# Keeping the split weights of the first MoE batch in DRAM and loading them for the other three

## The chip, the cores and the metric

The kernel runs on one core of one Trainium2 chip. A time is the device time of one execution in microseconds (us); what counts is the median over several executions.

## The reference

Three stages run one after the other. Attention with mixed heads makes x of 1792 tokens by 768 features. A dense "MoE" layer then computes g(x w_in) w_out with a hidden width of 2048, and a soft-MoE layer with 32 slots and 8 experts works on its output. The change lies in the second stage:

```python
def _moe_ref(x, w_in, w_out):
    h = x @ w_in            # 1792x768 @ 768x2048
    g = h - np.tanh(h)
    return g @ w_out        # 1792x2048 @ 2048x768
```

## The kernel before

**Attention** (`talking_heads`) runs until about 526 us. Beside it, the weights w_in and w_out, which arrive as 64-bit floats, are turned into 32-bit floats and stored in DRAM as 16 blocks `wi[f]` and 16 blocks `wo[f]`, each 128 partitions by 768 floats (384 KB).

**The MoE stage** (`moe_and_slots`) works on 4 batches of 448 tokens, and for each on the 16 blocks f of the hidden width: 64 steps t = 16b + f. A matmul is to be as exact as 32-bit floats need, but TensorE takes the fast format fp32r, so each operand is split into a high half (ScalarE copies it, rounded to fp32r) and a low half (what is left, by a subtraction), and three products are added: high by high, low by high, high by low. Both layers of a step therefore have 18 matmuls of 448 columns each.

- `stage1(t)` multiplies x by block `wi[f]` into the PSUM tile `hp` (L653); `gate(t)` computes g from it on ScalarE (`sq`, `qd`, `g`, L665 to L667) and VectorE (L668 to L673).
- `ready2(t)` splits `wo[f]` and g; `stage2(t)` multiplies them into the six accumulators `acc` (L686).
- `load_i` and `load_o` bring a block from DRAM on SyncE's queue (L600, L606). `split_to` makes the halves: the high one on ScalarE (L612), the low one on GpSimd for weights and on VectorE for g and x (L613). So each batch loads and splits the same 32 blocks again: 64 loads of `wi`, 64 of `wo`, 128 splits.

Every engine runs its instructions in the order in which the program writes them. In the middle of a batch a step t is written as: `load_i(t+2)`, `split_i(t+1)` (its names in the profile are `wir`, `wih`, `wil` for the raw block and its halves), `stage1(t)`, `gate(t)`, `stage2(t-2)`, then `ready2(t)` with the split of `wo` (`wor`, `woh`, `wol`) and `load_o(t+2)`. TensorE thus alternates stage1(t), stage2(t-2), stage1(t+1), stage2(t-1). The raw block of `wi` has one buffer, that of `wo` two, and each half has two.

At the start of batches 1 to 3 TensorE also finishes the batch before: `prep_logits`, `prep_transpose`, `prep_mix` and their like compute the slots of the soft MoE, mixed with the first four steps. At the end of a batch `split_x` splits the six blocks of the next x (`xh` on ScalarE, `xl` on VectorE).

From step 24 on, each step with a free tile also loads a piece of the expert weights (`load_expert`, L575, 1536 KB): seven pieces in steps 24 to 30, four in steps 53 to 56, two after the last stage1. The remaining experts are loaded while the last part (`hidden`, `finish`, `slot_out`, `output`) runs, from 1056 us to the end.

Of the kernel before, what the change touches and what calls it, by code (L numbers as in the profile page):

```python
# [16 lines left out]
NB, NH, SEQ, HD = 4, 12, 448, 64  # L17
# [23 lines left out]
def bits(ap):  # L41
    return ap.bitcast(FP32)
# [469 lines left out]
        pass  # L512


def moe_and_slots(tc, ident, xd, wi, wo, phi, w1, w2, out, box):
    nc = tc.nc
    NT, DM = out.shape
    KD = DM // 128
    NF = len(wi)
# [9 lines left out]
    steps = [(b, f) for b in range(NB) for f in range(NF)]  # L529
    NST = len(steps)  # L530
# [63 lines left out]
    raw_i, raw_o, wih, xraw, xhl, gt, ready, acc = {}, {}, {}, {}, {}, {}, {}, {}  # L594
    x2T, x2n, lp, es_in, runs = {}, {}, {}, {}, {}

    def load_i(t):
        if t < NST:
            a = xp.tile([128, DM], FP32, tag="wir", name="wir", bufs=1)
            nc.sync.dma_start(out=a, in_=wi[steps[t][1]])  # L600
            raw_i[t] = a

    def load_o(t):
        if t < NST:
            a = gt_p.tile([128, DM], FP32, tag="wor", name="wor")
            nc.sync.dma_start(out=a, in_=wo[steps[t][1]])  # L606
            raw_o[t] = a

    def split_to(pool, tag, n, src, lo_eng):
        h = pool.tile([128, n], F32R, tag=tag + "h", name=tag + "h", bufs=2)  # L610
        l = pool.tile([128, n], F32R, tag=tag + "l", name=tag + "l", bufs=2)
        nc.scalar.activation(out=h, in_=src, func=ACTF.Copy)  # L612
        lo_eng.tensor_tensor(out=l, in0=src, in1=bits(h), op=ALU.subtract)  # L613
        return h, l
# [24 lines left out]
    def stage1(t, mid=None):  # L639
        b, f = steps[t]  # L640
        if b and f == LAG - 1:
            hp = box["acc"].tile([128, SEQ], FP32, tag=f"a{KD - 1}", name="hp")
        else:
            hp = ph.tile([128, SEQ], FP32, tag="h", name="hp")
        wh, wl = wih.pop(t)
        n = 0
        for c in range(KD):
            if mid and c == KD // 2:
                mid()
            cs = slice(c * 128, (c + 1) * 128)  # L650
            xh, xl = xhl[b][c]
            for w, x in ((wh, xh), (wl, xh), (wh, xl)):
                nc.tensor.matmul(hp, lhsT=w[:, cs], rhs=x, start=(n == 0), stop=(n == 3 * KD - 1))  # L653
                n += 1
        return hp

# [19 lines left out]
    def stage2(t):  # L676
        b, f = steps[t]
        pa = box["acc"]
        if f == 0:
            for c in range(KD):  # L680
                acc[c] = pa.tile([128, SEQ], FP32, tag=f"a{c}", name="acc")
        wh, wl, gh, gl = ready.pop(t)
        for c in range(KD):
            cs = slice(c * 128, (c + 1) * 128)
            for i, (w, g) in enumerate(((wh, gh), (wl, gh), (wh, gl))):
                nc.tensor.matmul(  # L686
                    acc[c], lhsT=w[:, cs], rhs=g, start=(f == 0 and i == 0), stop=(f == NF - 1 and i == 2))
# [155 lines left out]
    pend = []  # L843

    def pop2():
        stage2(pend.pop(0))
        for u in pend[:2]:
            ready2(u)

    for t in range(NST):  # L850
# [55 lines left out]
    b = NB - 1  # L906
# [158 lines left out]
def fused_kernel(  # L1065
# [61 lines left out]
```

## Time and profile before

| | |
|---|---|
| median of 3 runs | 1159.91 us |
| lowest, highest | 1156.6, 1160.01 us |
| the profiled execution | 1161.43 us |
| its span in the profile | 1159.7 us |
| TensorE busy, share of the span | 1089.1 us, 94% |
| VectorE, ScalarE, GpSimd busy | 776.1, 655.2, 493.9 us |
| GpSimd: low halves of `wi`, of `wo` | 64 of 2.03 us, 64 of 1.90 us on average |
| bytes moved by DMA, mean rate | 221.08 MB, 191 GB/s |

The profile shows one execution. PE is TensorE's matmul, DVE VectorE, ACT ScalarE, POOL GpSimd, SP SyncE; "SPq" and "ACTq" are DMAs issued by SyncE and ScalarE. A busy TensorE is the bound only where its matmuls follow each other at their shortest distance, so the distance of one step to the next says more than the busy share.

### The profile page before, as it was taken

How to read it: one execution, taken by the hardware profiler on the slowest of the kernel's cores; microseconds unless marked ns; L12 is line 12 of the kernel's file. 1: busy time of each engine (PE TensorE's matmuls, PEld its weight loads, DVE VectorE, ACT ScalarE, POOL GpSimd, SP SyncE). 2: the span in 40 equal slices, each digit the busy share in tenths (PEclk: the TensorE clock that was granted, in tenths of full speed). 3: DMA queues.
4: the chain of work that ended last, by engine and by line, in shares of the span. 5: the costliest groups of instructions: out<-in, count | busy, mean ns of one | idle time of the engine just before them, and what ended most of it. 6: DMA issues, size and time to landing. Idle time of an engine off the chain costs nothing.

```text
span 1159.7 us, 20722 instructions
## 1 busy us (share of the span) xinstructions
PE 1089.1 (94%) x7208; PEld 871.5 (75%) x7208; DVE 776.1 (67%) x1428; ACT 655.2 (56%) x1399; POOL 493.9 (43%) x582
## 2 busy tenths in 40 slices
PE   7899999999998999999999899998999999999995
PEld 5677777777776777768888779886899879886443
DVE  6567666876767567636777787678966787775013
ACT  4777867867777677755454445445455554442022
POOL 1354455445644355545544345544455445450000
PEclk7899999999999899999999999999999999998898
DMA  5789868986899666544423224783333325627998
GB/s 121 193 233 238 239 188 243 253 228 201 231 240 233 205 204 216 178 151 140 150 95 110 69 82 157 270 293 103 131 111 107 97 68 195 240 83 272 365 388 308
DMA packets 160443, 221.08 MB, mean 191 GB/s; under 512 B 59124, under 2 KB 133172, under 8 KB 159828
## 3 DMA queue, kind: packets, MB, share of 16 engines
q1 hardware_dynamic: 160032, 219.65, 61.0%
q8 instruction: 58, 0.95, 0.3%
q14 instruction: 45, 0.37, 0.1%
q0 software_dynamic: 48, 0.10, 0.0%
q10 hardware_dynamic: 260, 0.01, 0.0%
HBM read 147.96 MB, written 23.59 MB: 148 GB/s over the span
## 4 chain that ended last, share of the span: by engine, by line
PE 47%; DVE 16%; DMA 14%; issue 8%; POOL 7%; ACT 7%; SPq 0%; POOLq 0%; DVEq 0%; ACTq 0%
PE tm L344 9%; PE pm L308 9%; PE acc L686 6%; PE vx L363 5%; DMA wir<-wi 5%; PE hp L653 5%; POOL wil L613 4%; DMA D<-S 3%; DVE qd L670 3%; PE sc L286 3%; PE sc L287 3%; DVE qd L668 2%; PE h L952 2%; DMA f<-in_moe_w_out_dram 2%; POOL wol L613 2%
## 5 line engine op out<-in xcount | busy, mean ns | idle before, releaser
L344 PEld LDWEIGHTS tm<-wk,e 120*112 120x112 f32 (+1 forms) x1440 | 171.7, 178 | 94.5 <-issue 55.9
L613 POOL TENSOR_TENSOR wil<-wir,wih 128x768 fp32r<-128x768 f32 x64 | 129.7, 2027 | 171.1 <-ACT wih L612 167.0
L344 PE MATMUL tm<-wk,e 120*112 120x120 f32 (+1 forms) x1440 | 180.2, 269 | 13.2 <-ACT aT L347 8.9
L310 DVE TENSOR_REDUCE mx<-pm 120x1 f32<-120x448 f32 x180 | 112.1, 623 | 113.3 <-PE pm L308 110.7
L334 POOL TENSOR_SCALAR wk<-wpost,rv 120x120 f32<-120x120 f32 x180 | 124.7, 693 | 137.5 <-PE tm L344 80.5
L308 PE MATMUL pm<-D,wpre 120*120 120x448 f32 x360 | 170.8, 556 | 7.6 <-DMA D<-S 2.5
L613 POOL TENSOR_TENSOR wol<-wor,woh 128x768 fp32r<-128x768 f32 x64 | 121.4, 1896 | 106.1 <-ACT woh L612 106.1
L347 ACT ACTIVATE aT<-tm 112x480 f32<-112x480 f32 x180 | 104.3, 580 | 103.6 <-PE tm L344 102.6
L653 PE MATMUL hp<-xh,wil 128*128 128x448 f32 x384 | 143.8, 374 | 7.3 <-POOL wil L613 7.0
L653 PE MATMUL hp<-xl,wih 128*128 128x448 f32 x384 | 141.8, 369 | 6.2 <-DVE xl L636 6.2
L653 PE MATMUL hp<-xh,wih 128*128 128x448 f32 x384 | 142.3, 371 | 4.4 <-ACT x2n L722 4.4
L686 PE MATMUL acc<-gh,woh 128*128 128x448 f32 x384 | 140.9, 367 | 0.0
L686 PE MATMUL acc<-gh,wol 128*128 128x448 f32 x384 | 140.6, 366 | 0.0
L686 PE MATMUL acc<-gl,woh 128*128 128x448 f32 x384 | 140.5, 366 | 0.0
L317 ACT ACTIVATE e<-pm,mx 120x448 f32<-120x448 f32 x180 | 112.5, 625 | 6.9 <-DVE rv L329 4.9
L668 DVE SCALAR_TENSOR_TENSOR qd<-qd,sq 128x448 f32<-128x448 f32 x64 | 57.5, 898 | 80.0 <-ACT qd L666 79.8
L612 ACT ACTIVATE gh<-g 128x448 fp32r<-128x448 f32 x64 | 36.8, 575 | 128.9 <-DVE g L673 127.1
L291 ACT ACTIVATE S<-sc 120x448 f32<-120x448 f32 (+1 forms) x188 | 100.7, 542 | 14.9 <-PE sc L287 7.2
L323 POOL TENSOR_SCALAR rv<-ss 120x1 f32<-120x1 f32 x180 | 46.3, 257 | 127.6 <-ACT e L317 119.8
L613 DVE TENSOR_TENSOR gl<-g,gh 128x448 fp32r<-128x448 f32 x64 | 73.0, 1144 | 36.2 <-ACT gh L612 36.2
L286 PE MATMUL sc<-khi,qT 128*120 128x448 f32 (+1 forms) x192 | 89.2, 464 | 7.4 <-ACT S L291 6.4
L653 PEld LDWEIGHTS hp<-xh,wil 128*128 128x128 f32 x384 | 72.4, 189 | 22.6 <-POOL wil L613 17.3
(135 smaller groups left out, 2017.6 us busy)
## 6 DMA issues: line engine op xcount, KB each, us to landing
ex<-in_moe_w_dram SPq DMA_DIRECT2D x32, 1536.0 KB
D<-S SPq DMA_DIRECT2D x172, 210.0 KB
wir<-wi SPq DMA_DIRECT2D x64, 384.0 KB
wor<-wo SPq DMA_DIRECT2D x64, 384.0 KB
f<-in_moe_w_in_dram SPq DMA_DIRECT2D x32, 384.0 KB
f<-in_moe_w_out_dram SPq DMA_DIRECT2D x32, 384.0 KB
wi<-fa SPq DMA_DIRECT2D x32, 192.0 KB
wo<-fa SPq DMA_DIRECT2D x32, 192.0 KB
```

The source lines that it names most:

```text
L286: nc.tensor.matmul(x[:ni], lhsT=qT[n][:, h, :ni], rhs=kT_hi[b, p][:, e, :], start=True, stop=False)
L291: nc.scalar.activation(out=S_t[n][:ni, h, :], in_=x[:ni], func=ACTF.Copy)
L308: nc.tensor.matmul(x[:r], lhsT=wpre[:r, :m, :], rhs=D_t.pop(s)[:r], start=True, stop=True)
L310: nc.vector.tensor_reduce(out=mx[:r], in_=x[:r], op=ALU.max, axis=AX.X, negate=True)
L317: nc.scalar.activation(out=e[:r], in_=pp_t.pop(s)[:r], func=ACTF.Exp, bias=mx_t.pop(s)[:r], accum_out=ss[:r])
L334: nc.gpsimd.tensor_scalar(out=wk[:r], in0=wpost[:r], scalar1=ss_t.pop(s)[:r], scalar2=None, op0=ALU.mult)
L344: nc.tensor.matmul(x[:, c, :, :m], lhsT=e[:r, c * JP:(c + 1) * JP], rhs=wk[:r, :, :m], start=True, stop=True)
L347: nc.scalar.activation(out=attn_t[n][:, :, :, c0:c0 + m], in_=x[:, :, :, :m], func=ACTF.Copy)
L613: lo_eng.tensor_tensor(out=l, in0=src, in1=bits(h), op=ALU.subtract)
L653: nc.tensor.matmul(hp, lhsT=w[:, cs], rhs=x, start=(n == 0), stop=(n == 3 * KD - 1))
L668: nc.vector.scalar_tensor_tensor(out=qd, in0=qd, scalar=TG_E, in1=sq, op0=ALU.add, op1=ALU.mult)
L686: nc.tensor.matmul(acc[c], lhsT=w[:, cs], rhs=g, start=(f == 0 and i == 0), stop=(f == NF - 1 and i == 2))
```

## The change

For batch 0 the raw block is loaded straight into the place of the low half of a tile that holds both halves. ScalarE writes the high half beside it, and GpSimd overwrites the raw block by the low half. One step later `save` stores both halves (768 KB) in DRAM, from ScalarE's queue. In batches 1 to 3 `load_i` and `load_o` bring both halves in one transfer of 768 KB, and no weight is split. The tile of `wi` has three buffers, that of `wo` two. Because a `wo` tile is now read by TensorE itself, its load is written behind `stage2(t-2)`, whose tile it takes, and no longer in `ready2`. In batches 1 to 3 the low half of g moves from VectorE to GpSimd.

```diff
+    WI_BUFS, WO_BUFS = 3, 2
+    unsaved = []
     def load_i(t):
         if t < NST:
-            a = xp.tile([128, DM], FP32, tag="wir", name="wir", bufs=1)
-            nc.sync.dma_start(out=a, in_=wi[steps[t][1]])
-            raw_i[t] = a
+            b, f = steps[t]
+            wih[t] = xp.tile([128, 2, DM], F32R, tag="wi", name="wi", bufs=WI_BUFS)
+            if b:
+                nc.sync.dma_start(out=bits(wih[t]), in_=wis[f])
+            else:
+                nc.sync.dma_start(out=bits(wih[t][:, 1]), in_=wi[f])
...
+    def split_to(w, kept):
+        raw = bits(w[:, 1])
+        nc.scalar.activation(out=w[:, 0], in_=raw, func=ACTF.Copy)
+        nc.gpsimd.tensor_tensor(out=w[:, 1], in0=raw, in1=bits(w[:, 0]), op=ALU.subtract)
+        unsaved.append((kept, w))
+
+    def save():
+        while unsaved:
+            kept, w = unsaved.pop(0)
+            nc.scalar.dma_start(out=kept, in_=bits(w))
     def split_i(t):
-        if t < NST:
-            wih[t] = split_to(xp, "wi", DM, raw_i.pop(t), nc.gpsimd)
+        if t < NF:
+            split_to(wih[t], wis[t])
     def ready2(t):
         if t in gt:
-            ready[t] = split_to(gp, "wo", DM, raw_o.pop(t), nc.gpsimd) + split_to(gp, "g", SEQ, gt.pop(t), nc.vector)
-            load_o(t + 2)
+            if t < NF:
+                split_to(woh[t], wos[t])
+            src = gt.pop(t)
...
+            nc.scalar.activation(out=h, in_=src, func=ACTF.Copy)
+            (nc.gpsimd if steps[t][0] else nc.vector).tensor_tensor(out=l, in0=src, in1=bits(h), op=ALU.subtract)
+            ready[t] = woh.pop(t), h, l
...
     def pop2():
-        stage2(pend.pop(0))
+        t = pend.pop(0)
+        stage2(t)
+        load_o(t + 2)
         for u in pend[:2]:
             ready2(u)
...
+        save()
         if t > 1:
             load_i(t + 2)
             split_i(t + 1)
```

`load_o` is changed like `load_i`, `stage1` and `stage2` read the halves out of the one tile, and `wis` and `wos` are 16 new DRAM blocks each. Three pieces of the engines' order show where the steps went. In each, the numbers behind a name count the program's buffers; a number right behind `wi`, `wo`, `wis` or `wos` in a source or target in DRAM is the block f.

ScalarE in the middle of batch 0, from the split of `wo` block 7 on. Before:

```order
L612 ACTIVATE woh_7429<-wor_7307 128x768
L612 ACTIVATE gh_7433<-g_7401 128x448
L612 ACTIVATE wih_7441<-wir_7374 128x768
L665 ACTIVATE sq_7464<-hp_7445 128x448
L666 ACTIVATE qd_7465<-sq_7464,tshift_6722 128x448
L667 ACTIVATE g_7466<-hp_7445 128x448
```

and now:

```order
L619 ACTIVATE wo_7440<-wo_7440 128x768
L639 ACTIVATE gh_7444<-g_7412 128x448
L626 DMA wis8_109<-wi_7324 128x1536
L626 DMA wos7_124<-wo_7440 128x1536
L619 ACTIVATE wi_7387<-wi_7387 128x768
L683 ACTIVATE sq_7473<-hp_7454 128x448
L684 ACTIVATE qd_7474<-sq_7473,tshift_6754 128x448
L685 ACTIVATE g_7475<-hp_7454 128x448
```

Two stores stand between the high half of g and the split of the next `wi` block. The second stores the `wo` tile whose low half GpSimd has just been given to make.

SyncE in the middle of batch 0, with the `wo` loads of blocks 6 to 8. Before:

```order
L606 DMA wor_7240<-wo6_91 128x768
L627 DMA xr_7242<-xd1_66 128x2688
L600 DMA wir_7244<-wi7_76 128x768
L606 DMA wor_7307<-wo7_92 128x768
L600 DMA wir_7309<-wi8_77 128x768
L606 DMA wor_7372<-wo8_93 128x768
```

and now:

```order
L615 DMA wo_7377<-wo6_91 128x768
L606 DMA wi_7387<-wi9_78 128x768
L615 DMA wo_7440<-wo7_92 128x768
L606 DMA wi_7450<-wi10_79 128x768
L615 DMA wo_7503<-wo8_93 128x768
L606 DMA wi_7513<-wi11_80 128x768
```

Measured in blocks, the `wi` loads run two blocks further ahead of the `wo` loads than they did.

SyncE where the first expert pieces are loaded, in batch 1. Before:

```order
L600 DMA wir_8612<-wi10_79 128x768
L606 DMA wor_8675<-wo10_95 128x768
L575 DMA ex_8677<-in_moe2_w1_dram 128x3x1024
L600 DMA wir_8679<-wi11_80 128x768
L606 DMA wor_8742<-wo11_96 128x768
L575 DMA ex_8744<-in_moe2_w1_dram 128x3x1024
```

and now:

```order
L604 DMA wi_8540<-wis10_111 128x1536
L613 DMA wo_8591<-wos8_125 128x1536
L575 DMA ex_8597<-in_moe2_w1_dram 128x3x1024
L604 DMA wi_8599<-wis11_112 128x1536
L613 DMA wo_8650<-wos9_126 128x1536
L575 DMA ex_8656<-in_moe2_w1_dram 128x3x1024
```

The order of the three kinds is kept, and the weight loads are twice as large.

## Rows read from the trace of the kernel before

**Rows 1.** Busy time by stretch: batches 0 to 3 of the MoE stage.
```profile
core 0: us, PE busy (x) PEld busy (x) DVE busy (x) ACT busy (x) POOL busy (x), PEclk, DMA share, GB/s
526.00:650.55 124.55, 121.59 (x667) 108.56 (x666) 91.36 (x117) 62.22 (x105) 58.98 (x33) 1.00 0.38 122
650.55:786.02 135.47, 129.42 (x644) 113.46 (x642) 101.46 (x138) 65.69 (x113) 63.10 (x32) 0.99 0.54 185
786.02:918.14 132.12, 126.50 (x644) 112.47 (x642) 100.03 (x143) 68.60 (x117) 66.61 (x33) 1.00 0.32 107
918.14:1056.25 138.11, 132.15 (x662) 115.27 (x660) 104.30 (x141) 62.75 (x108) 60.10 (x32) 1.00 0.45 152
```

**Rows 2.** Timeline of TensorE, batch 0: second matmul of stage1(5), stage1(15).
```profile
start us, us, engine line op out<-in xcount [idle before <-releaser]
560.81 0.47 PE L653 MATMUL hp<-xh,wil 128*128 128x448 f32 x1 [0.16 <-POOL wil L613]
...
639.50 0.47 PE L653 MATMUL hp<-xh,wil 128*128 128x448 f32 x1 [0.49 <-POOL wil L613]
```

**Rows 3.** Timeline of TensorE, batch 2: first matmul of two successive stage1.
```profile
856.13 0.36 PE L653 MATMUL hp<-xh,wih 128*128 128x448 f32 x1
...
863.42 0.37 PE L653 MATMUL hp<-xh,wih 128*128 128x448 f32 x1
```

**Rows 4.** Waits of TensorE from 651 to 1056 us: total, times, longest.
```profile
PE hp L653 <- DVE xl L636: 6.2, 6, 1.3
PE hp L653 <- ACT x2n L722: 4.4, 3, 1.5
PE hp L653 <- POOL wil L613: 4.1, 13, 0.8
```

**Rows 5.** Timeline of VectorE: one operation of `gate`, beside the prep and in mid-batch.
```profile
808.40 1.35 DVE L672 TENSOR_SCALAR sq<-sq 128x448 f32<-128x448 f32 x1
...
863.52 0.39 DVE L672 TENSOR_SCALAR sq<-sq 128x448 f32<-128x448 f32 x1
```

**Rows 6.** Timeline of SyncE and ScalarE: a `wir` load and what waited for it.
```profile
819.47 0.32 SPq L600 DMA_DIRECT2D wir<-wi  x1
...
822.44 0.85 ACT L612 ACTIVATE wih<-wir 128x768 fp32r<-128x768 f32 x1 [0.28 <-DMA wir<-wi]
```

**Rows 7.** Timeline of ScalarE and GpSimd in a step of batch 0.
```profile
584.07 0.85 ACT L612 ACTIVATE woh<-wor 128x768 fp32r<-128x768 f32 x1
...
585.00 1.85 POOL L613 TENSOR_TENSOR wol<-wor,woh 128x768 fp32r<-128x768 f32 x1 [0.62 <-ACT woh L612]
...
589.51 0.83 ACT L612 ACTIVATE wih<-wir 128x768 fp32r<-128x768 f32 x1
...
590.42 1.84 POOL L613 TENSOR_TENSOR wil<-wir,wih 128x768 fp32r<-128x768 f32 x1 [3.57 <-ACT wih L612]
```

**Rows 8.** A tile's instructions: a DMA issued by ScalarE (ns min, median, max).
```profile
L199 ACTq DMA_DIRECT2D wpostr<-in_w_post_dram x1: 795/795/795, 2.2 to 2.2; - x1
```

**Rows 9.** Busy time by stretch, columns as in rows 1.
```profile
735.00:780.00 45.00, 43.83 (x210) 38.75 (x210) 32.62 (x39) 19.39 (x32) 20.28 (x11) 1.00 0.87 307
1080.00:1120.00 40.00, 39.34 (x372) 19.98 (x368) 3.28 (x9) 6.49 (x17) 1.55 (x5) 0.93 1.05 391
1120.00:1145.00 25.00, 21.67 (x189) 9.92 (x181) 5.68 (x12) 5.43 (x11) 0.31 (x1) 1.00 0.98 351
```

**Rows 10.** DMA issues by line (queue, count, KB each).
```profile
ex<-in_moe_w_dram SPq DMA_DIRECT2D x32, 1536.0 KB
...
wir<-wi SPq DMA_DIRECT2D x64, 384.0 KB
```

**Rows 11.** DMA queues: packets, MB, share (q1 SyncE's, q10 ScalarE's).
```profile
q1 hardware_dynamic: 160032, 219.65, 61.0%
...
q10 hardware_dynamic: 260, 0.01, 0.0%
```

**Rows 12.** Timeline of SyncE at the end of the last batch.
```profile
1045.24 11.52 SPq L575 DMA_DIRECT2D ex<-in_moe_w_dram  x3
```

More of the change, by code (lines that the diff above doesn't have):

```diff
@@ L512, in talking_heads, with moe_and_slots @@
         pass
-def moe_and_slots(tc, ident, xd, wi, wo, phi, w1, w2, out, box):
+def moe_and_slots(tc, ident, xd, wi, wo, wis, wos, phi, w1, w2, out, box):
     nc = tc.nc
@@ L592, in moe_and_slots @@
     run_s = keep.tile([128, 1], FP32, tag="run_s", name="run_s")
-    raw_i, raw_o, wih, xraw, xhl, gt, ready, acc = {}, {}, {}, {}, {}, {}, {}, {}
+    wih, woh, xraw, xhl, gt, ready, acc = {}, {}, {}, {}, {}, {}, {}
+    WI_BUFS, WO_BUFS = 3, 2
+    unsaved = []
     x2T, x2n, lp, es_in, runs = {}, {}, {}, {}, {}
@@ L606, in load_o @@
[L606 to L614, printed above, removed]
+            b, f = steps[t]
+            woh[t] = gp.tile([128, 2, DM], F32R, tag="wo", name="wo", bufs=WO_BUFS)
@@ new lines, in load_o @@
+            if b:
+                nc.sync.dma_start(out=bits(woh[t]), in_=wos[f])
+            else:
+                nc.sync.dma_start(out=bits(woh[t][:, 1]), in_=wo[f])
+    def split_to(w, kept):
[7 more added lines that the diff above has]
+            nc.scalar.dma_start(out=kept, in_=bits(w))
@@ L616, in split_i @@
     def split_i(t):
-        if t < NST:
-            wih[t] = split_to(xp, "wi", DM, raw_i.pop(t), nc.gpsimd)
+        if t < NF:
+            split_to(wih[t], wis[t])
     def ready2(t):
         if t in gt:
-            ready[t] = split_to(gp, "wo", DM, raw_o.pop(t), nc.gpsimd) + split_to(gp, "g", SEQ, gt.pop(t), nc.vector)
-            load_o(t + 2)
+            if t < NF:
+                split_to(woh[t], wos[t])
+            src = gt.pop(t)
+            h = gp.tile([128, SEQ], F32R, tag="gh", name="gh", bufs=2)
+            l = gp.tile([128, SEQ], F32R, tag="gl", name="gl", bufs=2)
+            nc.scalar.activation(out=h, in_=src, func=ACTF.Copy)
+            (nc.gpsimd if steps[t][0] else nc.vector).tensor_tensor(out=l, in0=src, in1=bits(h), op=ALU.subtract)
+            ready[t] = woh.pop(t), h, l
@@ L651, in stage1 @@
             xh, xl = xhl[b][c]
-            for w, x in ((wh, xh), (wl, xh), (wh, xl)):
-                nc.tensor.matmul(hp, lhsT=w[:, cs], rhs=x, start=(n == 0), stop=(n == 3 * KD - 1))
+            for i, x in ((0, xh), (1, xh), (0, xl)):
+                nc.tensor.matmul(hp, lhsT=w[:, i, cs], rhs=x, start=(n == 0), stop=(n == 3 * KD - 1))
                 n += 1
@@ L681, in stage2 @@
                 acc[c] = pa.tile([128, SEQ], FP32, tag=f"a{c}", name="acc")
-        wh, wl, gh, gl = ready.pop(t)
+        w, gh, gl = ready.pop(t)
         for c in range(KD):
             cs = slice(c * 128, (c + 1) * 128)
-            for i, (w, g) in enumerate(((wh, gh), (wl, gh), (wh, gl))):
+            for i, (j, g) in enumerate(((0, gh), (1, gh), (0, gl))):
                 nc.tensor.matmul(
-                    acc[c], lhsT=w[:, cs], rhs=g, start=(f == 0 and i == 0), stop=(f == NF - 1 and i == 2))
+                    acc[c], lhsT=w[:, j, cs], rhs=g, start=(f == 0 and i == 0), stop=(f == NF - 1 and i == 2))
     def prep_evac(b):
@@ L1088, in fused_kernel @@
     wo = [dram.tile([128, DM], FP32, tag=f"wo{f}", name=f"wo{f}") for f in range(FF // 128)]
+    wis = [dram.tile([128, 2, DM], FP32, tag=f"wis{f}", name=f"wis{f}") for f in range(FF // 128)]
+    wos = [dram.tile([128, 2, DM], FP32, tag=f"wos{f}", name=f"wos{f}") for f in range(FF // 128)]
     order = [(f, hf, o) for f in range(FF // 128) for hf in range(2) for o in range(2)]
@@ L1096, in fused_kernel @@
             tc, ident, q, k, v, w_pre, w_post, xd, box,
-            lambda: moe_and_slots(tc, ident, xd, wi, wo, moe2_phi, moe2_w1, moe2_w2, out, box))
+            lambda: moe_and_slots(tc, ident, xd, wi, wo, wis, wos, moe2_phi, moe2_w1, moe2_w2, out, box))
 _INS = ['q', 'k', 'v', 'w_pre', 'w_post', 'moe_w_in', 'moe_w_out', 'moe2_phi', 'moe2_w1', 'moe2_w2']
```

4 lines of the change are left out of this document (2 added, 2 removed).

## The prediction

> **What bounds the kernel now.** I read the busy time by stretch first, then TensorE's timeline and its waits inside the stretches, then the chain of instructions that ends each wait, and last the DMA views. In each of the four batches TensorE is busy for all but 3 to 6 us [rows 1], so a change that only frees other engines can give back little. What TensorE needs at best is seen in batch 2: a step, 18 matmuls of each layer, takes 863.42 - 856.13 = 7.29 us with no gap [rows 3]. In batch 0 the second matmul of stage1(t), the first to read the low half `wil`, starts late in each step: ten steps take 639.50 - 560.81 us, 7.87 us each [rows 2]. So a step with such a wait costs 0.58 us more than one without. In batches 1 to 3 the waits of TensorE [rows 4] name three releasers: 13 times `wil` from GpSimd (4.1 us), 6 times the low half `xl` of x at the start of a batch (6.2 us), 3 times the copy `x2n` among the prep (4.4 us). The idle in these rows is less than the loss: 4.1 / 13 = 0.32 us of idle goes with 0.58 us of step, so each wait costs some 0.27 us more than it lists.
>
> **What goes, in batches 1 to 3.** The 96 weight splits leave ScalarE and GpSimd.
> - The waits for `wil`: 13 x 0.58 = 7.5 us.
> - The waits for `xl`: VectorE makes it, and VectorE is held up while a GpSimd split runs: the same operation took 1.35 us beside a split and 0.39 us without [rows 5]. At the start of batches 2 and 3 no split is left. At the start of batch 1 the split of the last `wo` block stays, so I keep one wait of 1.3 us. 6.2 + 6 x 0.27 - 1.3 - 0.3 = 6.2 us.
> - The waits for `x2n`: the copy stands on ScalarE behind the high half of g, which waits for VectorE's chain, and that chain holds one such stretched operation in each batch: 3 x (1.35 - 0.39) = 2.9 us.
>
> The sum is 16.6 us. Least would be the bare idle of `wil` and the `xl` idle without batch 1's two waits, 4.1 + 6.2 - 2.6 = 7.7 us. Most is all of TensorE's idle in the three stretches, 6.05 + 5.62 + 5.96 = 17.6 us [rows 1], with 0.27 us for each of the 22 waits listed, 23.6 us. I take 19 us, above the sum, because the prep's other waits hang on the same VectorE chain.
>
> The low half of g, now GpSimd's, costs nothing: by its width 448/768 x 1.85 = 1.1 us, and stage2(t) reads it one and a half steps (10.9 us) after gate(t). If it came late, it would show as a wait of `acc`.
>
> **What comes, in batch 0.** `load_o(t)` is moved behind stage2(t-2), because it now fills the tile that TensorE reads. From there a chain leads back to TensorE, since ScalarE keeps its order: `wo` split, high half of g, two stores, `wi` split. From the end of stage2(t-2):
> - the load, from its issue to the instruction that waits for it: 822.44 - 819.47 = 2.97 us [rows 6];
> - from the start of the high half to that of the low half: 585.00 - 584.07 = 0.93 us; the low half: 1.85 us [rows 7]; the store of `wo` waits for that low half;
> - the store's issue on ScalarE. No row shows it: SyncE's issues take 0.32 us [rows 6], one of ScalarE's, of another form, 0.80 us [rows 8]. I take 0.5 us;
> - the split of `wi` behind it: 590.42 - 589.51 = 0.91 us, and its low half 1.84 us [rows 7].
>
> That is 9.00 us until the second matmul of stage1(t+2) may start. Then 35 of the 36 matmuls of stage1(t+2) and stage2(t) are left, 35/36 x 7.29 = 7.09 us. So two steps take 16.1 us, 8.05 us each. The first store's issue hides under the wait for the low half. What is queued behind the waiting stores on ScalarE is the split of `wi` and the whole gate(t+1).
>
> The load is also slowed by what else moves. In batch 0 a step now loads 2 x 0.393 MB and stores 2 x 0.786 MB. Nothing in the trace shows stores beside loads from two queues: q1 carries nearly all [rows 11]. At 391 GB/s, the best rate of the trace [rows 9], both stores ahead of a load would delay it by 4.0 us; none would be 0. The second store is issued 5.75 us into a step of 8 us by the chain above, the next load 2.3 us later, so that about half of the 4.0 us has passed; two queues that share then delay the load by part of the rest. I take 0.8 us for each load, 0.4 us for each step, hence 8.45 us. The Trainium skill says in DMA: Bandwidth & Descriptors, section Issuing engines are not separate DMA queues, that DMAs from different engines run on the same 16 DMA engines and interleave, and that a second issuing engine only saves issue time. Worked out as an estimate of equal shares, a load of 1.0 us would take 2.0 us, and the step 8.55 us, 1.2 us more in the sum.
>
> Some 12 steps (4 to 15) run in this loop: 12 x (8.45 - 7.87) = 7 us. With 0.32 us for the issue and no delay a step is 7.96 us, and the term 1 us; with 0.8 us and one store ahead of the load (2.0 us) it is 9.2 us, and 16 us.
>
> **What comes, in batches 1 to 3.** A step loads 2 x 0.786 MB, twice what it loads now [rows 10], 215 GB/s, and a full load of 0.786 MB lands 2.97 + 1.0 = 4 us after its issue, where a `wo` tile has 10.9 us and a `wi` tile 14.6 us. That is hidden. It is not in the steps that also load an expert piece of 1.573 MB: 3.15 MB take 8.05 us at 391 GB/s, 0.76 us more than a step. Seven such steps run up 5.3 us against 14.6 - 8.05 - 1.97 = 4.6 us of lead of the `wi` tile: 0.7 us of loss, and none for the four in batch 3. At 351 GB/s [rows 9] a step takes 8.96 us: seven steps lose 11.7 - 3.7, four lose 6.7 - 3.7, 11 us in all. Today's expert steps moved 307 GB/s [rows 9], but no more was asked for. I take 3 us, near the best rate, as that row is a queue that was never empty. The Trainium skill gives in DMA: Bandwidth & Descriptors, section Specifications, an HBM limit of about 358 GB/s for one core; this trace shows 391 GB/s over 40 us, so the measurement decides. By the page's figure the term would be about 9 us.
>
> At the end, the first expert loads behind the last stage1 (at 1045.24 us now, [rows 12]) stand behind `load_o(63)`, which waits for one more layer (3.65 us) and moves 2.0 us of data ahead of them. The tail after 1056 us lives on such loads. Between 0 and 5.7 us; I take 1.5 us, as two pieces then have ten microseconds in which little else moves.
>
> **The sum:** -19 + 7 + 3 + 1.5 = -7.5 us. Against the profiled execution's 1161.4 us that is 1153.9 us; it lies 1.5 us above the median of the runs, so the forecast is 1152.5 us. A measurement of this kernel can tell 0.3%, 3.5 us, from no change.
>
> **Rivals.**
> - *Batch 0 becomes bound by ScalarE's stores (slower).* The store of `wo` waits for GpSimd with the `wi` split behind it, and the loads share the engines with 1.57 MB of stores for each step. For it: 2.36 MB for each step is near 300 GB/s, against 122 GB/s now [rows 1]. Against it: the stores have most of a step to drain. At 9.4 us for each step the term is 18.4 us, the time 1164 us. It decides the sign from a step of 9.1 us on (12 x 1.21 = 19 - 4.5).
> - *The expert steps become bound by DMA.* At 351 GB/s: 8 us more, 1160.5 us.
> - *The waits stay.* If only the least gain of 7.7 us comes, the time is 1164 us. Against it: the releasers that the waits name are these splits, and VectorE beside them [rows 4, 5].
> - *It is all cheaper:* 23.6 us gained and the lower ends of the costs (1, 0.7, 0) give 1138 us; half way to it is 1145 us.
>
> **How the numbers follow.** The forecast has a chance of 0.5, its own range is 1147 to 1158 us; the stores 0.17, DMA 0.1, the waits that stay 0.08, cheaper 0.15. Faster by over 0.3% are four fifths of the forecast, the cheap case and a little of the rest: 0.56. Within 0.3% lie the rest of the forecast, most of the DMA case and parts of the others: 0.22. Slower: 0.22. The range of 1142 to 1166 us leaves out the best of the cheap case and the worst of the stores.
>
> **What would show it.** Right: TensorE's steps at 7.29 us throughout batches 1 to 3, no wait for `xl` at the start of batches 2 and 3; in batch 0 steps of 8.2 to 8.7 us, with the second matmul of stage1 released by GpSimd, and ScalarE's second store released by GpSimd. Wrong: waits of TensorE for `wi` or `wo` loads outside steps 28 to 33, steps above 9.1 us in batch 0, or a batch 0 as long as before.

## The result, and the profile after

| | before | after |
|---|---|---|
| median of 20 runs | 1161.72 us | 1151.79 us |
| lowest, highest | 1155.1, 1172.92 us | 1146.16, 1156.76 us |
| the profiled execution | 1161.43 us | 1156.76 us |
| batch 0, from its first stage1 to that of batch 1, profiled execution | 124.4 us | 135.8 us |
| stage1(16) to stage1(63), in batches 1 to 3, profiled execution | 390.0 us | 369.0 us |

The ratio of the times is 0.9914, 95% interval [0.9896, 0.9933]; a second measurement (e12) gave 0.9938 [0.9916, 0.996]. The change is faster by 0.6 to 0.9%. The profiled execution of after is the longest of its 20, so it shows 4.7 us of gain where the medians show 9.9.

Busy time by stretch of the kernel after, batches 0 to 3, columns as in [rows 1]:

```profile
core 0: us, PE busy (x) PEld busy (x) DVE busy (x) ACT busy (x) POOL busy (x), PEclk, DMA share, GB/s
528.92:664.77 135.85, 124.65 (x666) 110.51 (x664) 89.04 (x119) 61.61 (x102) 56.24 (x31) 0.97 0.78 291
664.77:793.15 128.38, 125.53 (x643) 112.59 (x642) 67.84 (x128) 43.89 (x83) 22.14 (x17) 1.00 0.76 291
793.15:919.08 125.93, 125.29 (x644) 112.69 (x642) 63.42 (x121) 42.97 (x82) 18.52 (x16) 1.00 0.59 218
919.08:1049.46 130.38, 129.01 (x661) 115.86 (x660) 64.39 (x124) 41.26 (x78) 19.00 (x18) 1.00 0.65 244
```

Against [rows 1] batch 0 is 11.5 us longer (124.36 between the same marks before; the row there begins 0.2 us early) and batches 1 to 3 are 7.1, 6.2 and 7.7 us shorter, 21.0 us in all. What is left of the sum: the attention ahead of them took 2.7 us more, though nothing in it was changed, and the tail 2.1 us more. 2.7 + 11.5 - 21.0 + 2.1 = -4.7 us. These are differences of two single executions. In the fourteen kernels traced for this document the attention, the same in all, ended between 520 and 529 us; the kernel before was traced once.

Waits of TensorE in the kernel after, from 526 to 1056 us (total, times, longest), beside [rows 4]:

```profile
PE hp L671 <- POOL wi L620: 9.4, 9, 1.4
PE acc L704 <- ACT gh L639: 1.8, 1, 1.8
PE hp L671 <- ACT x2n L740: 1.7, 3, 0.6
PE hp L671 <- ACT wi L619: 1.7, 1, 1.7
...
PE acc L704 <- DMA wo<-wos: 0.8, 1, 0.8
```

The waits for `xl` and, in batches 1 to 3, those for GpSimd's low half of `wi` are gone; all nine `wi` waits now lie in batch 0. In the traces of e1, e6, e8, e9 and e12, which have the same batches 1 to 3, some wait for `xl` stays at the start of batch 1, 0.3 to 2.4 us.

Batch 0 has two parts. Measured between the starts of stage1 on TensorE, stage1(0) to stage1(8) took 66.2 us (57.6 before), stage1(8) to stage1(15) 57.4 us (54.8), and the last stretch to stage1(16) 12.3 us (11.9). The first, which no term of the prediction has, is the larger. Timeline of the kernel after, SyncE, ScalarE and TensorE in steps 4 and 5:

```profile
552.49 0.33 ACTq L626 DMA_DIRECT2D wis<-wi  x1
...
552.85 2.17 ACTq L626 DMA_DIRECT2D wos<-wo  x2
...
557.80 0.32 SPq L615 DMA_DIRECT2D wo<-wo  x1
...
562.73 0.84 ACT L619 ACTIVATE wo<-wo 128x768 fp32r<-128x768 f32 x1 [5.25 <-DMA wo<-wo]
...
566.88 0.47 PE L671 MATMUL hp<-xh,wi 128*128 128x448 f32 x1 [1.65 <-ACT wi L619]
568.77 0.74 PE L671 MATMUL hp<-xh,wi 128*128 128x448 f32 x1 [1.42 <-POOL wi L620]
```

and the waits of SyncE's queue from 530 to 650 us:

```profile
SPq L615 <- PE acc L704: 81.9, 11, 12.0
SPq L615 <- DMA wos<-wo: 14.4, 3, 8.2
```

TensorE was done with the `wo` tile at 555.97 us, but its next load is issued at 557.80 us: the store of that tile, issued at 552.85 us, had not landed. The load then takes 4.93 us instead of 2.97 [rows 6], and ScalarE stands behind it for 5.25 us. Three loads wait for a store, 5.0, 8.2 and 1.2 us of the queue's time, but only in the one shown, the longest, does the store hold the load, by those 1.8 us: in the other two TensorE lets the tile go later than the store (loads issued at 548.67 and 565.30 us). When TensorE goes on, its clock is down:

```profile
564.00:568.00 4.00, 1.70 (x8) 0.98 (x6) 1.96 (x2) 2.02 (x5) 2.64 (x2) 0.93 0.75 227
568.00:572.00 4.00, 3.23 (x9) 2.89 (x10) 3.97 (x5) 1.24 (x2) 2.20 (x2) 0.50 1.00 416
572.00:576.00 4.00, 4.00 (x16) 3.62 (x15) 1.88 (x3) 2.31 (x4) 1.18 (x2) 0.72 1.00 414
```

After 1.65 and 1.42 us of idle the granted clock is 0.50, the level of 1.2 GHz, and 15 matmuls follow each other at 0.37 us instead of 0.20, which costs 15 x 0.17 = 2.6 us.

A steady step of batch 0 looks as the prediction drew it (timeline of the kernel after, ScalarE, GpSimd and SyncE):

```profile
611.77 0.32 SPq L615 DMA_DIRECT2D wo<-wo  x1
...
614.90 0.85 ACT L619 ACTIVATE wo<-wo 128x768 fp32r<-128x768 f32 x1 [3.34 <-issue]
615.24 0.33 ACTq L626 DMA_DIRECT2D wis<-wi  x1
...
615.88 1.84 POOL L620 TENSOR_TENSOR wo<-wo 128x768 fp32r<-128x768 f32 x1 [3.96 <-ACT wo L619]
617.75 0.33 ACTq L626 DMA_DIRECT2D wos<-wo  x1
618.13 0.84 ACT L619 ACTIVATE wi<-wi 128x768 fp32r<-128x768 f32 x1 [1.91 <-POOL wo L620]
...
619.05 1.81 POOL L620 TENSOR_TENSOR wi<-wi 128x768 fp32r<-128x768 f32 x1 [1.33 <-ACT wi L619]
```

The load, 3.13 us, the low half of `wo`, the store that waits for it, then the `wi` split, whose low half TensorE needs.

### The profile page after: what moved, and what is told of

The parts are those of the page before. It is cut to its first block, busy times and chain, and to the rows that moved or that the text cites. A ratio compares the mean times of both kernels' runs of the same rounds, so it can differ in the third digit from the quotient of the medians.

```text
span 1155.0 us, 20495 instructions
## 1 busy us (share of the span) xinstructions
PE 1086.2 (94%) x7208; PEld 874.5 (76%) x7208; DVE 663.9 (57%) x1380; ACT 586.4 (51%) x1303; POOL 361.8 (31%) x534
## 4 chain that ended last, share of the span: by engine, by line
PE 75%; DMA 9%; ACT 4%; DVE 4%; POOL 4%; issue 3%; ACTq 0%; SPq 0%; POOLq 0%; DVEq 0%
PE hp L671 18%; PE acc L704 17%; PE tm L344 9%; PE pm L308 9%; PE vx L363 6%; DMA D<-S 4%; PE sc L286 3%; PE sc L287 3%; DMA ex<-in_moe_w_dram 2%; PE so L1002 2%; PE h L974 2%; POOL wo L620 1%; POOL wi L620 1%; PE tz L991 1%; DMA f<-in_moe_w_in_dram 1%
## 5 line engine op out<-in xcount | busy, mean ns | idle before, releaser
L671 PE MATMUL hp<-xh,wi 128*128 128x448 f32 x768 | 224.7, 372 | 12.9 <-POOL wi L620 9.4
L704 PE MATMUL acc<-gh,wo 128*128 128x448 f32 x768 | 218.8, 366 | 3.1 <-ACT gh L639 1.8
L671 PEld LDWEIGHTS hp<-xh,wi 128*128 128x128 f32 x768 | 144.5, 190 | 31.8 <-POOL wi L620 13.3
L704 PEld LDWEIGHTS acc<-gh,wo 128*128 128x128 f32 x768 | 144.0, 188 | 16.0 <-ACT gh L639 2.2
L640 POOL TENSOR_TENSOR gl<-g,gh 128x448 fp32r<-128x448 f32 x48 | 55.5, 1155 | 319.5 <-ACT gh L639 256.8
L671 PE MATMUL hp<-xl,wi 128*128 128x448 f32 x384 | 141.3, 368 | 0.0
L704 PE MATMUL acc<-gl,wo 128*128 128x448 f32 x384 | 140.3, 365 | 0.0
L683 ACT ACTIVATE sq<-hp 128x448 f32<-128x448 f32 x64 | 34.6, 540 | 92.2 <-PE hp L671 73.0
L363 PEld LDWEIGHTS vx<-aT,vn 112*64 112x64 f32 x1536 | 73.8, 137 | 9.0 <-DVE f L61 3.0
L363 PE MATMUL vx<-aT,vn 112*64 112x120 f32 (+1 forms) x1536 | 80.5, 261 | 0.0
```

The lines of the kernel that those rows point to most:

```text
L363: nc.tensor.matmul(x[64 * e:64 * e + 64, i, :ni], lhsT=nat_v[b, hf][:, h, c, :], rhs=a[:, c, NP * hf + h, :ni], start=(c == 0), stop=(c == ...
L640: (nc.gpsimd if steps[t][0] else nc.vector).tensor_tensor(out=l, in0=src, in1=bits(h), op=ALU.subtract)
L671: nc.tensor.matmul(hp, lhsT=w[:, i, cs], rhs=x, start=(n == 0), stop=(n == 3 * KD - 1))
L704: nc.tensor.matmul(acc[c], lhsT=w[:, j, cs], rhs=g, start=(f == 0 and i == 0), stop=(f == NF - 1 and i == 2))
```

## The experiments

All figures of batch 0 are distances of stage1 starts: "start" is stage1(0) to (8), "seven steps" (8) to (15). Six executions hold the changed kernel's batch 0 untouched (after, e3, e4, e5, e7, e12): start 62.4 to 69.3, mean 65.2 us; seven steps 57.4 to 58.4 us; batch 0 132.1 to 139.6, mean 135.4 us. From stage1(16) to (63) the six with batches 1 to 3 untouched (after, e1, e6, e8, e9, e12) took 369.0 to 372.1 us, mean 370.6; after is the shortest of them. What is smaller than this spread is not read from one execution. Ratios are to the kernel before on the same chip.

**e1: the stores of batch 0 behind the next `wi` split.**

```diff
-        save()
+        due = len(unsaved)
         if t > 1:
             load_i(t + 2)
             split_i(t + 1)
+        save(due)
```

> Only the place of the two stores of batch 0 in ScalarE's order moves, from ahead of the next wi split to behind it. Theory (the loss of 11.5 us in batch 0 is a wait in order: load of wo, wo split, GpSimd's low half, store waiting for it on ScalarE, wi split): the wi low half then follows the wo low half at once on GpSimd, so from stage2(t-2) it is 3.1 + 0.93 + 1.84 + 1.84 = 7.7 us, with 7.09 us of matmuls 14.8 us for two steps, and a step takes 7.4 us instead of 8.22; batch 0 shrinks by 6 to 8 us from 135.85 us, the whole to about 1145 us. Rival (the stores' traffic beside the loads costs it): bytes are the same, so steps stay at 8.0 to 8.3 us and the whole at 1150 to 1153 us.

Measured: 1150.81 us, ratio 0.9913 [0.988, 0.9946]; start 63.6, seven steps 55.6, batch 0 131.2 us. The seven steps are 2 us shorter, so the place of the store in ScalarE's order did cost them; but they stop at the 54.8 us of the kernel before and not at 7.4 us each. Twelve `wo` loads now wait for the later store (25.0 us of SyncE's queue together, 3 times in after). Half a hit: the whole is no faster than the changed kernel's that can be told.

**e2: no stores.** Batches 1 to 3 read the raw block twice, so the output differs and the bytes loaded do not.

```diff
-            nc.scalar.dma_start(out=kept, in_=bits(w))
+            pass
...
-                nc.sync.dma_start(out=bits(wih[t]), in_=wis[f])
+                nc.sync.dma_start(out=bits(wih[t]), in_=wi[f].unsqueeze(1).to_broadcast([128, 2, DM]))
```

> Batch 0 stores nothing; batches 1 to 3 read the raw block twice into the two halves of the tile, 768 KB as before, so their loads have the same size and the output is not the reference's. Theory (order): a step of batch 0 takes 7.3 to 7.4 us, as with the stores moved behind the split, so the two runs agree within 1 us in the steady steps. Rival (traffic): the steady steps are shorter here than with the stores moved, by up to 0.8 us each. The bump of some 7 us at steps 4 and 5, where wo loads took 3.9 and 5.3 us of waiting: gone here if the stores' traffic makes it, still here if it is only the start of the same loop. Whole: 1145 us if only the steady steps change, 1138 us if the bump goes too.

Measured: 1141.78 us, ratio 0.9832 [0.9779, 0.9884]; start 58.3, seven steps 55.2, batch 0 124.9 us, as before the change. The seven steps agree with e1 within 0.5 us: there it is order. They stay at 7.9 us each, where 7.3 to 7.4 was expected. The start falls by 7 us: there it is the stores, by their landing, their traffic or their issues. The `wo` load behind stage2, which this kernel keeps, costs nothing that can be seen by itself. (From stage1(30) to (32) this kernel took 24.8 us against 20.3 in after, so its whole understates what batch 0 gained.)

**e6: the raw `wo` block of batch 0 in a tile of its own.**

```diff
+                raw_o[t] = gt_p.tile([128, DM], FP32, tag="wor", name="wor", bufs=1)
+                nc.sync.dma_start(out=raw_o[t], in_=wo[f])
...
+                split_to(woh[t], wos[t], raw_o.pop(t))
+                if t + 1 < NF:
+                    load_o(t + 1)
```

> In batch 0 the raw wo block has a tile of its own again (one buffer), loaded right behind the split of the block before, and no longer behind stage2(t-2). The stores stay where they are. Theory (the chain begins with the load's place): the load of about 3 us leaves the chain, 5.9 + 7.09 = 13 us for two steps, less than TensorE's 14.6, so steps take 7.3 to 7.4 us; the wo loads at the start are early too, so the bump goes: batch 0 shrinks by 10 to 15 us from 135.85 us, the whole to 1137 to 1142 us. Rival (the stores, their issue on ScalarE or their traffic, cost it wherever the load stands): steps stay above 7.9 us, whole 1149 to 1153 us.

Measured: 1147.4 us, ratio 0.988 [0.9827, 0.9933]; start 66.4, seven steps 55.2, batch 0 132.7 us. Again the steady loss goes, so the load's place is part of the chain; but a step is 7.9 us, not 7.3 to 7.4, and the start stays, so the theory misses. Only block 0 is loaded ahead here: the second raw load goes out behind the split of the first, at 537.63 us, into the burst of the first stores, and ScalarE has it at 545.06 us. Whether that is why the start stays is what e8 asks. TensorE's clock fell here too, to 0.50 from 556 to 560 us.

**e5: expert pieces in every second step.**

```diff
-        if t >= 24:
+        if t >= 24 and t % 2 == 0 or t >= 53:
```

> The seven expert pieces of steps 24 to 30 are loaded in every second step, 24 to 36. Theory (the one stall of batch 1, 1.8 us at stage2(30), is its wo tile late behind expert pieces, though the profile names the copy gh): the stall is gone, batch 1 shrinks from 128.4 to 126.5 us, the whole by 2 us, which is at the edge of what the runs tell. Rival (it really is gh, late behind the engines' work): the stall stays at 1.5 to 2 us and batch 1 at 128 us. If later pieces delay other loads, a new stall shows between steps 31 and 38.

Measured: 1150.71 us, ratio 0.9921 [0.9896, 0.9945]. The stretch from stage1(30) to stage1(32) took 18.2 us instead of 20.3, and no wait is left there. The theory holds, against the name that the profile gives. The kernel after, timeline of SyncE and TensorE at that place:

```profile
780.35 0.32 SPq L613 DMA_DIRECT2D wo<-wos  x1
780.72 0.44 SPq L575 DMA_DIRECT2D ex<-in_moe_w_dram  x1
...
789.44 0.64 PE L704 MATMUL acc<-gh,wo 128*128 128x448 f32 x2 [1.83 <-ACT gh L639]
```

The matmul waits for several semaphores; with the pieces spread out, `gh` unchanged, the wait is gone. It was the `wo` load behind the pieces. Other executions of the same loads name it outright (waits of TensorE in e12, the same kernel, from 526 to 1056 us; 0.8 us of it at stage2(63)):

```profile
PE acc L704 <- DMA wo<-wos: 2.7, 2, 1.8
```

The stretch took 20.1 to 22.8 us in the six executions with batches 1 to 3 untouched, so the stall is worth 1.9 to 4.5 us and after had one of the smallest. All three kernels with the pieces spread (e5, e11, e13) took 18.2 us. They pay a part of it back as the expectation warned, at the end of the spread pieces: the step from stage1(38) took 8.3 to 8.5 us instead of 7.3. Timeline of e13, TensorE:

```profile
839.14 0.64 PE L712 MATMUL acc<-gh,wo 128*128 128x448 f32 x2 [0.94 <-DMA wo<-wos]
```

**e3: GpSimd's work back in batches 1 to 3**, on a tile that nobody reads, once for each block of `wi` and of `wo` up to step 59.

```diff
+        elif t < NST - 4:
+            nc.gpsimd.tensor_tensor(out=spin, in0=spin, in1=spin, op=ALU.subtract)
```

> Batches 1 to 3 get GpSimd's work back without its use: one subtraction of 128x768 floats where each wi split stood and one where each wo split stood, on a tile that nobody reads, so that nothing waits for it but what stands behind it on GpSimd. Theory (part of the gain came since GpSimd's splits held up VectorE): VectorE's operation of gate goes back to some 1.3 us where it meets one, the waits for xl and x2n come back, and batches 1 to 3 lose 5 to 11 us of the 21 us gained; the gl half now stands behind the subtractions and may add waits of acc. The part of the wil waits (7.5 us by the prediction) stays gained. Rival (the gain came from ScalarE's freed time, or from the wil waits alone): under 2 us lost.

Measured: 1164.42 us, ratio 1.0058 [1.0024, 1.0091], 12 us above e4 on the same chip and slower than the kernel before. From stage1(16) to (63) it is 379.4 us, 10.4 above after and 7.3 above the longest of the six with batches 1 to 3 untouched. VectorE in batches 1 to 3 (660 to 1040 us), mean ns of one operation, the kernel before:

```profile
L670 DVE SCALAR_TENSOR_TENSOR qd<-sq,qd 128x448 f32<-128x448 f32 x46 | 46.4, 1009 | 0.0
...
L672 DVE TENSOR_SCALAR sq<-sq 128x448 f32<-128x448 f32 x46 | 30.6, 665 | 0.0
...
L636 DVE TENSOR_TENSOR xl<-xr,xh 128x448 fp32r<-128x448 f32 x12 | 13.1, 1162 | 0.0
```

the kernel after:

```profile
L687 DVE TENSOR_TENSOR g<-hp,g 128x448 f32<-128x448 f32 x49 | 30.2, 617 | 0.0
L688 DVE SCALAR_TENSOR_TENSOR qd<-sq,qd 128x448 f32<-128x448 f32 x49 | 30.1, 615 | 0.0
...
L654 DVE TENSOR_TENSOR xl<-xr,xh 128x448 fp32r<-128x448 f32 x18 | 11.8, 719 | 0.0
```

and e3:

```profile
L693 DVE SCALAR_TENSOR_TENSOR qd<-sq,qd 128x448 f32<-128x448 f32 x47 | 47.0, 1000 | 0.0
...
L692 DVE TENSOR_TENSOR g<-hp,g 128x448 f32<-128x448 f32 x47 | 28.9, 615 | 0.0
L659 DVE TENSOR_TENSOR xl<-xr,xh 128x448 fp32r<-128x448 f32 x16 | 20.0, 1315 | 0.0
```

The work of GpSimd alone, which nothing reads, stretches `qd` from 615 to 1000 ns and `xl` from 719 to 1315, as in the kernel before. It does not bring back the stretched `sq`: 426 ns here, 412 in after, 665 before. So e3 is not the old load in full.

Not all of the 10.4 us is what the theory means. Some 5 us lie in the first steps of the batches (3.6) and in the prep (1.5), where VectorE's chain counts, and 1.7 in the stall at stage2(30), which varies by more than that. The other 3.7 lie in steps in which TensorE waits for nothing and each matmul is 2% further from the next, with the granted clock printed as 1.00. Timeline of e3, TensorE, first matmuls of two successive stage1, 7.44 us apart:

```profile
848.47 0.57 PE L676 MATMUL hp<-xh,wi 128*128 128x448 f32 x2
...
855.91 0.57 PE L676 MATMUL hp<-xh,wi 128*128 128x448 f32 x2
```

e5 has such steps without any added work, so they can't be put down to GpSimd. The profiled execution is the shortest of the ten of e3, so where the longer ones lose more it doesn't show.

**e4: ScalarE's work back**, the same with a copy on ScalarE.

```diff
+        elif t < NST - 4:
+            nc.scalar.activation(out=spin, in_=spin, func=ACTF.Copy)
```

> The same with ScalarE's work: one copy of 128x768 floats where each high half was made in batches 1 to 3, on a tile that nobody reads. Theory (GpSimd and VectorE, not ScalarE, made the waits): under 2 us lost of the 21 us, since ScalarE is idle half the time there. Rival (ScalarE's copies delayed gate and the prep): 4 us or more lost, most of it in the first five steps of each batch.

Measured: 1152.26 us, ratio 0.9934 [0.9906, 0.9962]; stage1(16) to (63) 369.9 us, 0.9 us above after and inside the spread of the six. The theory holds.

**e7: the low half of g on VectorE.**

```diff
-            (nc.gpsimd if steps[t][0] else nc.vector).tensor_tensor(out=l, in0=src, in1=bits(h), op=ALU.subtract)
+            nc.vector.tensor_tensor(out=l, in0=src, in1=bits(h), op=ALU.subtract)
```

> The low half of g is made by VectorE in all batches, as in the kernel before. Theory (this part of the change is worth nothing): batches 1 to 3 within 1.5 us of the changed kernel's 384.7 us, since without splits GpSimd holds up VectorE no more and each step leaves VectorE idle. Rival (the move to GpSimd carried a part of the gain): batches 1 to 3 longer by 3 us or more, with waits for xl or x2n back.

Measured: 1148.13 us, ratio 0.9898 [0.985, 0.9945]; stage1(16) to (63) 370.9 us, and the 1.9 us above after, inside the spread of the six, stand in batch 1's expert steps. This part of the change is worth nothing that can be seen.

**e8: blocks 0 to 2 of `wo` loaded ahead**, e6 with the first two in the halves' tile.

```diff
+            if t < 2:
+                woh[t] = gp.tile([128, 2, DM], F32R, tag="wo", name="wo", bufs=WO_BUFS)
+                nc.sync.dma_start(out=bits(woh[t][:, 1]), in_=wo[f])
...
     load_o(1)
+    load_o(2)
```

> As with the raw wo block in a tile of its own, but blocks 0 and 1 go straight into the halves' tile as in the changed kernel, and block 2 is loaded into the raw tile ahead, with them. So no wo load of batch 0 waits for a store that reads its tile, and none stands behind a wi load that does before step 3. Theory (the start of batch 0, 66.2 us from stage1(0) to stage1(8) against 57.6 before, is lost since three wo loads wait 5.0, 8.2 and 1.2 us for the landing of the stores that read their tiles): start 58 to 61 us, steady steps 7.9 us, batch 0 126 to 128 us, the whole 1141 to 1145 us. Rival (the burst of stores fills the DMA engines, share 1.0, and delays whatever is loaded): start 63 to 67 us as in the runs so far, whole 1147 us.

Measured: 1147.87 us, ratio 0.9909 [0.988, 0.9937]; start 63.6, seven steps 57.3, batch 0 133.0 us. The theory misses: no `wo` load waits for a store in this trace, and the start is as long as in the executions with batch 0 untouched. The rival's times came, but e13 speaks against its reason. In the steady steps another wait has come up: with the raw block early, ScalarE splits `wo` at once and then stands 4.15 us before the high half of g, which waits for VectorE; the two store issues and the `wi` split come behind that, in every step. The chain has changed its head and kept its length. What holds the start here was not found.

**e9: the `wi` split ahead of all that**, right behind gate(t).

```diff
-            split_i(t + 1)
...
             gate(t, hps.pop(t))
+            split_i(t + 2)
```

> One line moves: the split of wi block t+2 is written right behind gate(t), ahead of wo's split, the high half of g and the stores, and no longer behind them. Theory (what holds TensorE in batch 0, in the kernel before too, is the place of the wi split in ScalarE's order: behind gh, which waits for VectorE's chain, and now also behind the wo load and two stores): seven steady steps take 51 to 53 us instead of 57.4, less than the 54.8 of the kernel before; the start from stage1(0) to stage1(8) falls from 62 to 69 us, as the runs so far had it, to 58 to 62; the whole 1140 to 1144 us. Rival (the wo load behind stage2(t-2), its split and low half bound the loop through stage2 as well, or the DMA traffic does): seven steps stay at 55 us or more, the whole at 1147 us or more.

Measured: 1153.05 us, ratio 0.992 [0.9891, 0.9948]; start 62.7, seven steps 53.9, to stage1(16) 15.5 (12.3 after), batch 0 132.1 us. The steps fall by 3.5 us or more against the untouched executions, so the order was a part of what held them; they are the first below those of the kernel before, by 0.9 us, which is no more than their spread. They don't reach 53 us, and the time is the same. In SyncE's queue another wait has grown, 545 to 650 us:

```profile
SPq L615 <- DMA wos<-wo: 85.2, 14, 11.5
```

Fourteen `wo` loads, not three, wait for the store of their tile to land. That TensorE's waits in this batch come from there is likely but not shown; the profile names VectorE's `g` for most of them (5.4 us, 5 times).

**e11: e8 and e9 together, expert pieces spread, x of batch 1 loaded later.**

```diff
+        if f == LAG + (1 if b else 6) and b + 1 < NB:
...
+            split_i(t + 2)
...
+        if t >= 24 and t % 2 == 0 or t >= 53:
```

> The early wi split, the raw wo tile loaded ahead, the expert pieces in every second step, and the load of x for batch 1 five steps later (f = 10 instead of 5 in batch 0). Theory: batch 0 at 117 to 122 us, the stall of 2 us in batch 1 gone, the whole 1136 to 1141 us, below both kernels. Rival (the first stores fill the DMA engines whatever the order): the start stays at 62 us or more, batch 0 above 124 us, and this is no faster than the early split alone.

Measured: 1184.87 us, ratio 1.0213 [1.0178, 1.0247]; seven steps 83.5, batch 0 167.6 us. A clear miss, made by the combination. Timeline of e11, SyncE and ScalarE:

```profile
603.80 0.32 SPq L619 DMA_DIRECT2D wor<-wo  x1
...
604.22 0.42 SPq L606 DMA_DIRECT2D wi<-wi  x1
609.98 0.84 ACT L623 ACTIVATE wi<-wi 128x768 fp32r<-128x768 f32 x1 [4.09 <-DMA wi<-wi]
...
614.90 0.32 SPq L619 DMA_DIRECT2D wor<-wo  x1
```

On SyncE the `wi` load stands behind the raw `wo` load, which waits for GpSimd to be done with the block before; on ScalarE that block's split stands behind the `wi` split, which waits for the `wi` load. Each step runs once round this loop, 11.1 us.

**e12: the changed kernel again**, as the base of e9 and e11; nothing edited.

> The changed kernel itself, on the same chip as the two above, as their base. Both theories: 1150 to 1153 us; batch 0 between 132 and 140 us, as in the four runs so far that have its batch 0 unchanged.

Measured: 1154.45 us, ratio 0.9938 [0.9916, 0.996], 1.5 us above the range; start 67.1, seven steps 58.4, batch 0 137.8 us. On this chip e9's 1153.05 us are no gain that can be told.

**e13: e11 with the orders put right.** Nothing waits behind a wait: in step t SyncE loads `wi` of block t + 3, then the raw `wo` block; ScalarE does gate(t), the stores, the `wi` split, then the `wo` split.

```diff
+            load_i(t + 3)
             gate(t, hps.pop(t))
+            save()
+            split_i(t + 2)
```

> The raw wo tile loaded ahead, with each engine's order rearranged so that nothing waits behind a wait: wi of block t+3 is loaded right behind stage1(t), ahead of the raw wo block on SyncE's queue; then gate(t), the stores of the step before, the split of wi block t+2, and last the split of wo. Expert pieces in every second step, x of batch 1 loaded at f = 10. Theory (batch 0 was held by waits that stand in front of other work on SyncE and ScalarE, the last one being the wi load behind the raw wo load): seven steady steps 51 to 54 us, no wait of a wo or wi load for a store in the steady steps, start 58 to 63 us, batch 0 at 122 to 128 us, the stall of batch 1 gone; the whole 1138 to 1144 us, below both kernels. Rival (the stores beside the loads hold it through the DMA engines): steady steps 55 us or more, batch 0 above 131 us, the whole at 1148 us or more.

Measured: 1145.66 us, ratio 0.9861 [0.9819, 0.9903]; start 55.9, seven steps 59.7, to stage1(16) 17.4, batch 0 133.1 us. It has the lowest median of the kernels that compute the reference, and is clearly below the one before; against the changed kernel its interval lies below e12's and overlaps that of the 20 runs, and it overlaps those of e1 and e5 to e9 too. Batch 0 is only 2.3 us below the mean of the untouched ones, and much of the rest lies elsewhere: against e12, 3.6 us in the expert stretch and 3.8 in the tail, which was not aimed at. The steady steps and batch 0 came as the rival had them. The start settles a question: the five steps from stage1(3) to stage1(8) are 7.3 us each, at a clock of 1.00 and with the DMA engines as full as in after (share 0.84 in these five steps, 0.78 in after's). From 540 to 560 us:

```profile
540.00:544.00 4.00, 4.00 (x22) 3.70 (x21) 3.93 (x6) 1.58 (x2) 2.35 (x2) 1.00 1.05 350
544.00:548.00 4.00, 4.00 (x22) 3.70 (x21) 3.02 (x6) 3.47 (x6) 1.95 (x2) 1.00 0.98 368
...
556.00:560.00 4.00, 4.00 (x22) 3.70 (x21) 3.18 (x3) 2.85 (x5) 2.27 (x2) 1.00 0.96 397
```

So stores and full DMA engines beside the loads cost nothing while the loads have a lead. (The load of x for batch 1 has moved out of this stretch too; no run moves it alone.) From stage1(8) on the lead is used up (timeline of e13, SyncE and ScalarE):

```profile
593.44 0.33 ACTq L630 DMA_DIRECT2D wis<-wi  x1
...
594.46 0.32 SPq L619 DMA_DIRECT2D wor<-wo  x1
594.46 0.35 ACTq L630 DMA_DIRECT2D wos<-wo  x1
...
599.84 0.85 ACT L623 ACTIVATE wo<-wor 128x768 fp32r<-128x768 f32 x1 [4.12 <-DMA wor<-wo]
```

The one raw tile is loaded again only when GpSimd has read it, and beside two stores of the same moment the load takes 5.38 us, not 2.97. With the split (0.95 us to GpSimd's start) and the low half, 1.85 us, the loop is 8.2 us, near the steps' 8.5. A second raw tile, which would let the next load start earlier, was not tried.

## Why the prediction was right, and where it was off

The forecast, 1152.5 us, and the sign were right. The closeness, 0.7 us, is in part luck: the gain and the cost of batch 0 were both taken too small and cancelled, and the forecast stands on three runs of the kernel before whose median was 1.8 us below that of twenty. The gain was forecast as 7.5 us and measured as 9.9.

- **Batches 1 to 3, taken as -19 us, with the expert steps apart.** Measured: 21.0 us less in after, 17.9 to 21.0 over the six executions of these batches; without the stall at stage2(30), 21 to 23 us, just below the stated bound of 23.6. By place, from stage1 starts before and after: first step of the batch 4.0, 3.4 and 0.9, together 8.4 us (6.2 for the `xl` waits; 6.3 to 8.8 in the other five of those six); the prep in the four steps behind it 2.3, 2.8 and 2.5, together 7.6 us (2.9 for `x2n`); the steps in mid-batch 5.1 + 2.0 for the stall = 7.1 us (7.5 for `wil`). The step that was mis-sized is the `x2n` one, "3 x (1.35 - 0.39) = 2.9 us": it priced one stretched operation for each batch, and the prep gave back 2.3 to 2.8 us in each. The surcharge to 19 us covered half of that. Of the cause, e3 and e4 show that GpSimd's work, read by nobody, takes back 12 us in the median and ScalarE's nothing that can be told. The trace of e3 puts 5 us of this where the prediction had it, in the waits behind VectorE's chain, and little of it in the prep. That the rest of the gain is the halves' being ready early is inferred; no run tests it by itself.
- **Batch 0, taken as +7 us.** Measured: 11.5 us, 8 to 15 us over six executions, mean 11.0, against one execution before. The steady chain was right in its links and too dear in its size: 8.2 us for a step in after, against 7.83 before (54.8 / 7), so 0.4 us and not 0.58 a step. A store's issue took 0.33 us, not 0.5, and the load 3.13 us, not 2.97 + 0.8. What the sum lacks is the start: 8.5 of the 11.5 us were lost there, 2.6 of them by the lower clock. The step that failed is "From the end of stage2(t-2)", which lets the `wo` load start there: such a load must also wait for the store that reads its tile. In steady steps that has landed; at the start, with several stores queued, it had not, which held one load by 1.8 us, and the same load was stretched by 2.0 us. But these waits are not the whole of it: e8 takes them away and the start stays. That the stores cost the start, e2 shows; by which way most of it, stays open.
- **That batch 0 would be bound by the stores** did not come: the twelve steps from 4 on lost 0.9 us each on average, of the 1.2 us that would have decided the sign. But the stores are what cost, as e2 shows, and e13 shows a start at full speed with the DMA engines as full, so it is not by filling them.
- **Expert steps, +3 us.** 2.0 us at stage2(30) in after, 1.9 to 4.5 us over the six executions of batches 1 to 3, mean 3.1; the wait was for a load, as e5 shows, at 375 GB/s in that stretch (734 to 790 us). That is above the 358 GB/s by which the prediction worked out 9 us beside its sum.
- **Tail, +1.5 us.** 2.1 us in after, 0.2 to 2.4 over the same six; stage2(63) waited 0.8 us for its load, and the first expert loads went out behind it.
- **GpSimd's low half of g, nothing.** e7 agrees.

What was to show it did: steps of 7.3 us in batches 1 to 3, no `xl` waits at the start of batches 2 and 3, batch 0's second matmul released by GpSimd and the second store too, steady steps of 8.2 us. Two signs of the other kind came as well: steps above 9.1 us in batch 0, all in the start (10.9, 11.6 and 9.2 us), and a wait for a `wo` load outside steps 28 to 33, 0.8 us at stage2(63).

## What to carry to other kernels

A tile is busy until the last store out of it has landed, so a store added to a ring of two buffers can make the next load wait for a transfer; count readers by DMA like readers by an engine, at the start, where transfers queue, above all. Read a stall from several executions before you size it: the one at stage2(30) was 1.9 us in one and 4.5 in another. On an engine that keeps its order, look for what can wait and put it last: moving one wait away here brought up the next four times, and an order changed on one queue alone made a loop. And before explaining a wait by the instruction that the profile names, remove the other candidate.

## What the hardware showed that was not expected

- Beside GpSimd's subtraction VectorE's `qd` from `sq` and `qd`, and `xl`, both with operands in SBUF only, took 1.6 and 1.8 times as long (e3), the other `qd` 1.2 times; `g` from `hp`, which lies in PSUM, kept its 615 to 617 ns. The Trainium skill has the rule in SBUF — State Buffer, section SBUF: two separate sides: a GpSimd operation that reads SBUF and a VectorE operation with two SBUF inputs exclude each other from a shared port pair for a whole instruction. The trace agrees in which operations are held; the size is the measured one.
- A load of 384 KB that took 2.97 us by itself took 4.93 us (after) and 5.38 us (e13) beside stores from ScalarE's queue. That fits the Trainium skill, DMA: Bandwidth & Descriptors, section Issuing engines are not separate DMA queues: both use the same 16 engines.
- With no wait at all and the granted clock printed as 1.00, steps took 7.44 us instead of 7.29 in some stretches (e5, from 849 to 908 us; e3, in the middle of batches 2 and 3). Two of the fourteen traces have it. Why stays open.
